# Attention and mixture of experts: key columns of z tile by tile, moving side in blocks of 32, stored squares read back in two transfers, other lags in the planner

## The chip, the cores and the metric

One core of one Trainium2 chip runs the kernel. The metric is the device time of one execution in microseconds (us). Before the change it is 2173.44 us, the median of three runs (2169.32 to 2173.81).

## The reference

Eight batches of 2496 tokens pass an attention without softmax and then a mixture of eight experts:

```python
scores = scale * np.matmul(z, z.transpose(0, 2, 1))      # scale = 1 / S, z is S x 64
attn = np.maximum(scores, 0.0) ** 2
out = np.matmul(attn, v)                                 # v is S x 256
x = (u * out).reshape(B * S, D)

logits = x @ w_gate + modality_bias[modality_id]
e_idx = np.argmax(logits, axis=1)                        # one expert a token
out[mask] = gate_w[mask, None] * (np.maximum(x[mask] @ w1[e], 0.0) @ w2[e])
```

Everything is single precision. The scores are symmetric, because both sides of the product are z.

## The kernel before

The kernel has two parts. The first does the attention of all batches and sends each token's row to a list of its expert in DRAM (`xs`). The second takes tiles of 512 rows from these lists and runs them through the expert's two matrices. The change touches only the first part, which ends about 1279 us into the span. Where single precision is wanted, a tile is split into a high and a low part (`ah` and `al`, `vh` and `vl`, the two halves of `zm`), and three matmuls are made of one.

**Tiles and steps.** A batch has 20 tiles of 128 keys and five chunks of queries, four of 512 and one of 448. A step (b, c, i) weighs the pair i of key tiles for query chunk c of batch b, so a chunk has ten steps and a batch fifty. Keys are grouped in chunks of four tiles as well. In a full step these instructions run:

- `scores` (L318): six matmuls on TensorE of 64 rows each, for two key tiles with three products of high and low parts. They are issued in pairs: the two of a pair use the two halves of the array's rows and run at the same time. The stationary side is 128 key columns of `zm`, given by `key_columns`; the moving side is the 512 query columns.
- `root` (L326) and `square` (L372) on ScalarE: the scores leave PSUM through a Relu and are squared, giving the tile `r`.
- `high` (L396) makes `ah` on ScalarE or VectorE, `low` (L405) makes `al` on VectorE.
- `weigh` (L429): 24 matmuls on TensorE, which add the squares times v to the chunk's four PSUM banks `acc` (two halves of the rows by two halves dh of the 256 columns). The first eight need `ah` and `vh`, the next `ah` and `vl`, the last `al` and `vh`.

**Squares used twice.** By symmetry, the squares of query chunk c and key chunk q with q > c are those of query chunk q and key chunk c, turned. So in a step whose keys lie in a later chunk, `turn_squares` (L343, VectorE) turns the 1024 elements in blocks of 32 x 32, and `store_squares` (L355, L359) sends them to DRAM in four transfers (six in the last pair). Later `load_turned` (L335) brings them back as the tile `r` of 158 steps, which then have no scores, root or square. A step of 242 in all has scores of its own.

**Key columns.** The host writes z with its tokens reordered. In the kernel before, two key tiles share 256 columns and alternate: tile j takes every second column. Only the last key chunk's third and fourth tile (pair i = 9) lie as 128 adjacent columns. The queries are read as 512 adjacent columns.

**The end of a chunk.** `evacuate_low` (L485, ScalarE) and `evacuate_high` (L489, VectorE) take the four `acc` banks into the rows tile `x`, multiplication by u follows (L496), then the rows are split in three bf16 parts `rb` (L508, L514, L510), turned on TensorE by `make_rows` (L525, two groups of 24 row-tiled pairs of short matmuls, in PSUM tiles `po`) and copied back (L535, L536). PSUM has two banks for one score tile and six others; four of the six hold `acc`, and the next chunk's first `weigh` needs four that the evacuation gives free. It is therefore made in two halves: first dh = 0, then dh = 1.

**What sets the order.** The whole first part is laid out by a planner in the kernel's Python code. Each piece of work has an engine, an assumed duration, a due time counted in steps (`need`), the pieces it comes after with a lag each (`after`), and the buffers that it takes and gives free. The planner walks the engines' assumed clocks and gives each engine the piece that is due first among those that are ready. The result is a fixed order on every engine. On the chip each engine then runs its list in order, and waits where an operand isn't there yet. All loads and stores of the first part go through one queue, issued by SyncE (SP), and each transfer waits for the one issued eight places earlier to have landed.

Of the kernel before, what the change touches and what calls it, by code (L numbers as in the profile page):

```python
# [11 lines left out]
I32 = mybir.dt.int32  # L12
# [15 lines left out]
def tile_attention_moe(ctx: ExitStack, tc: tile.TileContext, ut, v, zt, mid, wg, mb, w1, w2, out):  # L28
# [99 lines left out]
    n = NCOL - J  # L128
    nc.gpsimd.iota(toki[:, 0:n], pattern=[[T, NCH - 1], [1, J]], base=0, channel_multiplier=J)
    nc.gpsimd.iota(toki[:, n:NCOL - 1], pattern=[[1, J - 1]], base=n * P, channel_multiplier=J - 1)  # L130
# [64 lines left out]
    def load_modality():  # L195
        nc.sync.dma_start(out=brow, in_=mb.rearrange("(o m) e -> o m e", o=1).broadcast_to([P, 2, E]))
        mi = raw.tile([P, B, NCOL, 2], I32, tag="mi", name="mi")
        nc.gpsimd.memset(mi, 0)
        small_raw["mi"] = mi
        mid32 = mid.bitcast(I32).rearrange("(b s w) -> b s w", b=B, w=2)  # L200
        for c in range(NCH - 1):
            nc.sync.dma_start(
                out=mi[:, :, c * J:(c + 1) * J, :].rearrange("p b j w -> p b (j w)"),
                in_=mid32[:, c * T:(c + 1) * T, :].rearrange("b (p j) w -> p b (j w)", j=J),
            )
        c0, c1 = (NCH - 1) * J, NCOL - 1
        nc.sync.dma_start(
            out=mi[:, :, c0:c1, :].rearrange("p b j w -> p b (j w)"),
            in_=mid32[:, c0 * P:S - 64, :].rearrange("b (p j) w -> p b (j w)", j=J - 1),
        )  # L210
        nc.sync.dma_start(out=mi[0:64, :, c1, :], in_=mid32[:, S - 64:S, :].rearrange("b p w -> p b w"))

# [75 lines left out]
    steps = [(b, c, i) for b in range(B) for c in range(NCH) for i in order_of(b, c)]  # L288
    first_step = {(b, c): order_of(b, c)[0] for b in range(B) for c in range(NCH)}
    st_s, st_a, st_h, st_t = {}, {}, {}, {}  # L290
    acc = {}

    def key_columns(x, k):

        c, j = k // J, k % J
        if c == NCH - 1 and j >= J // 2:
            return x[:, j * P:(j + 1) * P]
        return x[:, j // 2 * H:(j // 2 + 1) * H].rearrange("p (k n) -> p n k", n=2)[:, j % 2]

# [4 lines left out]
    def scores(g, more=False):  # L304

        b, c, i = steps[g]
        w = width[c]
        if more:
            s = [bank_tile([P, T], "s") for _ in halves]
        else:  # L310
            both = ps_s.tile([P, 2, T], F32, tag="s", name="s")
            s = [both[:, t, :] for t in range(2)]
        mv = Z[b, c]
        for n, (kl, ql) in enumerate(((0, 1), (1, 0), (0, 0)) if g else ((0, 0), (0, 1), (1, 0))):
            for t in range(2):
                k = 2 * i + t
                lhs = key_columns(Z[b, k // J][halves[t], kl], k)
                nc.tensor.matmul(out=s[t][:, :w], lhsT=lhs, rhs=mv[halves[t], ql, :w], start=n == 0, stop=n == 2)  # L318
        st_s[g] = s if more or not g else both
# [9 lines left out]
    def load_turned(g):  # L329

        b, c, i = steps[g]
        w = width[c]
        a = bulk.tile([P, 2, T], F32, tag="a", bufs=NA, name="r")
        src = squares[i // 2, c, b % 2].rearrange("(s p k) q -> s p k q", s=2, k=2)
        nc.sync.dma_start(out=a[:, :, :w], in_=src[i % 2, :, :, :w])  # L335
        st_a[g] = a

    def turn_squares(g):

        b, c, i = steps[g]  # L340
        y = raw.tile([P, T // BLK, 2 * BLK], F32, tag="turn", bufs=2, name="turn")
        order = "p t (i n) -> p n t i" if i < NI - 1 else "p t (n i) -> p n t i"
        nc.vector.transpose(out=y.rearrange(order, n=2), in_=st_a[g].rearrange("p n (t i) -> p n t i", i=BLK))  # L343
        st_t[g] = y
# [173 lines left out]
    def make_rows(b, c, n):  # L518

        parts = turned_rows[b, c] = [bank_tile([P, J // 2, KD, DK + GW], "po") for _ in halves]  # L520
        for j in range(J // 2):
            for dh in range(KD):
                for m, x in enumerate(parted[b, c]):
                    for y, h in zip(parts, halves):
                        nc.tensor.matmul(  # L525
                            out=y[:, j, dh, :], lhsT=x[h, n * J // 2 + j, dh * P:(dh + 1) * P], rhs=mover[h, dh, :],
                            start=m == 0, stop=m == NP - 1,
                        )

    def take_rows(b, c, n, r):  # L530

        y = turned_rows[b, c][r]
# [368 lines left out]
    def piece(on, us, need, f, *args, after=(), take=(), drop=(), gate=-1):  # L901
        p = Piece(on, us, need, f, args, [d if isinstance(d, tuple) else (d, 0.1) for d in after if d], list(take), drop, gate)
        pieces.append(p)
        return p
# [26 lines left out]
    def z_pieces(b, c):  # L931
        need = uses_z[b, c][0] - LEAD
        read = None
        if b:
            hold_zr[b, c] = Hold("zr")
            read = transfer(0.7, need - 4, load_z, b, c, take=[hold_zr[b, c]], gate=need - 25)
        high = piece("A", 0.55, need - 1, prep_z_high, b, c, after=[read], take=[hold_z[b, c]], gate=int(need - 4))
        done_z[b, c] = piece("D", 0.65, need - 0.6, prep_z_low, b, c, after=[high], drop=[hold_zr[b, c]])
        begun.append(done_z[b, c])

    def v_pieces(b, c):
        need = uses_v[b, c][0]
        read = high = None
        if b or c == NCH - 1:
            if b:
                hold_vr[b, c] = Hold("vr")
            read = transfer(1.4, need - 5, load_v, b, c, issues=3 if c == NCH - 1 else 1, take=[hold_vr[b, c]], gate=need - 25)
        if (b, c) != (0, 1):
            high = piece("A", 0.95, need - 1.5, prep_v_high, b, c, after=[read], take=hold_v[b, c][:1])
        done_v[b, c] = piece("D", 1.15, need - 1.2, prep_v_low, b, c, after=[high], take=hold_v[b, c][1:], drop=[hold_vr[b, c]])  # L950
# [9 lines left out]
    def step_pieces(n):  # L960
# [4 lines left out]
        if is_turned(n):  # L965
            src = [stored[b, i // 2, 2 * c + k] for k in range(2)]
            p = transfer(1.4, n - LEAD - 2.5, load_turned, n, after=src, take=[hold_a], gate=n - LEAD - 4)
            high_after = (p, 0.2)
# [38 lines left out]
        if first and n:  # L1007
            p = piece("P", us / 2, n, weigh, n, 0, after=ready, take=own[0])
            p = piece("P", us / 2, n, weigh, n, 1, after=[(p, 0.0)], take=own[1], drop=hold_h + v_of)
        else:  # L1010
# [3 lines left out]

    acc_hold, later = {}, []

    def chunk_pieces(b, c):
# [7 lines left out]
        for h in range(KD):  # L1025
            lows.append(piece(
                "A", 0.5 * f + 0.06, end - 0.6, evacuate_low, b, c, h, after=[(w, 0.25)] + lows[:1], drop=[own[h][1]],
                take=[] if h else [hold_x[b, c]],
            ))
# [3 lines left out]
        for h in reversed(range(KD)):  # L1033
            highs.append(piece("D", 0.6 * f + 0.06, end - 0.4, evacuate_high, b, c, h, after=[lows[1]] + highs[:1], drop=[own[h][0]]))
        x = piece("D", 1.18, end + 1.5, weigh_u, b, c, after=[highs[1], read], drop=[hold_u[b, c]])
# [7 lines left out]
        for k in range(2):  # L1043
            own = [Hold("bank"), Hold("bank")]
            p = piece("P", 0.62, end + 3.4 + 0.3 * k, make_rows, b, c, k, after=[(p, 0.15), done_once["gate"]], take=own, drop=parts_of[:1] if k else [])
            took += [piece("A", 0.42, end + 3.6 + 0.3 * k, take_rows, b, c, k, r, after=[(p, 0.25)] + took[-1:], drop=own[r:r + 1]) for r in range(2)]
# [28 lines left out]
    done_once["gate"] = piece("D", 0.9, 7, prep_gate, after=[p])  # L1075
    p = transfer(2.0, 8, load_modality, issues=7, gate=6)
    done_once["modality"] = piece("D", 1.5, 20, prep_modality, after=[(p, 2.0)], gate=12)
# [416 lines left out]
```

## Time and profile before

| | |
|---|---|
| median of three runs | 2173.44 us (2169.32 to 2173.81) |
| profiled execution | 2171.07 us, span 2169.1 us |
| TensorE matmul busy | 2144.8 us (99%) |
| VectorE busy | 1653.8 us (76%) |
| ScalarE busy | 1456.9 us (67%) |
| granted TensorE clock | 0.998 |
| moved by DMA | 373.70 MB |

All views are of one execution. "Busy" for TensorE is the union of its matmuls, which overlap, so a busy engine can still be slower than it might be. A row of waits has the waiting engine, tile and line, what it waited for, and then the total in us, how often, and the longest. A row of the timeline has the start and the length in us, the engine (PE is TensorE's matmuls, PEld its weight loads, DVE VectorE, ACT ScalarE, POOL GpSimd, SPq the transfers issued by SP), the line, and how many instructions were merged. A row of the windows gives, for a stretch of the span, the busy time of PE, PEld, DVE, ACT and POOL with instruction counts, the granted clock, the busy share of the DMA engines, and GB/s. A row of grouped instructions ends with the count, the busy time in us and the mean of one in ns, and then the engine's idle time before them.

### The profile page before, as it was taken

The numbers are of one execution on the slowest core, as the hardware profiler recorded it, in microseconds if no ns is written. First come the engines' busy times: TensorE is split into PE (matmuls) and PEld (weight loads), VectorE is DVE, ScalarE is ACT, GpSimd is POOL, SyncE is SP. The second block draws the span as 40 slices with busy tenths as digits, with TensorE's granted clock in tenths as the row PEclk, the third lists the DMA queues.
The fourth block names the chain that finished last, engine by engine and source line by source line (L and its number), as shares of the span: only waits on it lengthen the run. The fifth ranks groups of instructions, "written<-read, shape, count | busy, mean of one in ns | idle before, by whom it ended". The sixth has DMA issues, their size and how long they took to land.

```text
span 2169.1 us, 44305 instructions
## 1 busy us (share of the span) xinstructions
PE 2144.8 (99%) x17190; PEld 1835.2 (85%) x17190; DVE 1653.8 (76%) x2260; ACT 1456.9 (67%) x2032; POOL 363.3 (17%) x342
## 2 busy tenths in 40 slices
PE   9999999999999999999999999999999999999997
PEld 7888888898889888888888988888888888888886
DVE  8888889789889788888788866666666666666664
ACT  8779779779778778778788653555455545555553
POOL 0000300300300301301302404121111212111121
PEclk9999999999999999999999999999999999999999
DMA  8976976967957957957957834554454535455450
GB/s 179 257 210 125 247 222 138 254 207 156 277 171 170 291 152 177 300 146 159 284 124 161 215 101 128 153 147 145 129 164 124 168 117 157 135 140 152 127 158 24
DMA packets 587878, 373.70 MB, mean 172 GB/s; under 512 B 488426, under 2 KB 543210, under 8 KB 581898
## 3 DMA queue, kind: packets, MB, share of 16 engines
q1 hardware_dynamic: 572570, 329.58, 59.3%
q0 software_dynamic: 15088, 41.21, 5.1%
q8 instruction: 136, 2.23, 0.4%
q14 instruction: 84, 0.69, 0.1%
HBM read 246.49 MB, written 140.96 MB: 179 GB/s over the span
## 4 chain that ended last, share of the span: by engine, by line
PE 48%; issue 26%; DMA 13%; DVE 4%; POOL 3%; SPq 3%; ACT 3%; POOLq 0%; DVEq 0%; ACTq 0%
PE acc L429 38%; DMA out_dram<-y,ids 10%; PE s L318 6%; POOL out_dram L1261 3%; PE po L525 2%; SPq L355 2%; DMA r<-squares 2%; PE ph L1238 1%; DVE al L405 1%; ACT r L326 1%; PE po L1251 1%; ACT r L372 1%; DMA squares<-turn 1%; DVE turn L343 1%; ACT ah L396 0%
## 5 line engine op out<-in xcount | busy, mean ns | idle before, releaser
L429 PE MATMUL acc<-ah,vh 64*128 64x512 f32 (+1 forms) x3120 | 455.3, 385 | 4.0 <-ACT x L485 3.1
L405 DVE TENSOR_TENSOR al<-r,ah 128x1024 fp32r<-128x1024 f32 (+1 forms) x359 | 422.2, 1187 | 36.0 <-ACT ah L396 30.3
L1251 PE MATMUL po<-w,hh 128*128 128x512 f32 x1248 | 445.8, 393 | 0.0
L429 PE MATMUL acc<-al,vh 64*128 64x512 f32 (+1 forms) x3120 | 443.9, 382 | 0.0
L429 PE MATMUL acc<-ah,vl 64*128 64x512 f32 (+1 forms) x3120 | 442.2, 382 | 0.0
L1242 ACT ACTIVATE hh<-ph 128x512 fp32r<-128x512 f32 x312 | 186.4, 597 | 376.8 <-PE ph L1238 337.0
L1238 PE MATMUL ph<-xh,w 128*128 128x512 f32 x1248 | 427.5, 393 | 0.0
L1243 DVE SCALAR_TENSOR_TENSOR hl<-ph,hh 128x512 fp32r<-128x512 f32 x312 | 215.7, 691 | 225.9 <-ACT hh L1242 192.7
L649 POOL DMA_INDIRECT xs<-x,sloti x160 | 205.6, 1285 | 1055.0 <-issue 501.7
L429 PEld LDWEIGHTS acc<-ah,vh 64*128 64x128 f32 x3120 | 319.8, 184 | 51.8 <-ACT x L485 5.4
L429 PEld LDWEIGHTS acc<-al,vh 64*128 64x128 f32 x3120 | 322.5, 184 | 41.9 <-DVE al L405 0.3
L429 PEld LDWEIGHTS acc<-ah,vl 64*128 64x128 f32 x3120 | 316.0, 184 | 42.8
L1252 PE MATMUL po<-w,hl 128*128 128x256 f32 x1248 | 348.6, 279 | 0.0
L396 ACT CAST ah<-r 128x1024 fp32r<-128x1024 f32 (+1 forms) x282 | 287.8, 1034 | 52.9 <-DMA r<-squares 28.5
L326 ACT ACTIVATE r<-s 128x1024 f32<-128x1024 f32 (+2 forms) x244 | 248.9, 1021 | 68.7 <-PE s L318 60.9
L1238 PEld LDWEIGHTS ph<-xh,w 128*128 128x128 f32 x1248 | 234.7, 188 | 54.0 <-PE acc L429 0.3
L1251 PEld LDWEIGHTS po<-w,hh 128*128 128x128 f32 x1248 | 234.3, 188 | 54.2
L1261 POOL DMA_INDIRECT out_dram<-y,ids x157 | 153.1, 975 | 741.0 <-DVE y L1289 702.6
L343 DVE STREAM_TRANSPOSE turn<-r 128x1024 f32<-128x1024 f32 x158 | 196.2, 1242 | 83.1 <-DMA squares<-turn 38.9
L372 ACT ACTIVATE r<-r 128x1024 f32<-128x1024 f32 (+2 forms) x243 | 255.7, 1053 | 5.4
L1238 PE MATMUL ph<-xl,w 128*128 128x512 f32 x624 | 245.6, 394 | 0.3 <-DVE xl L875 0.3
L1252 PEld LDWEIGHTS po<-w,hl 128*128 128x128 f32 x1248 | 234.2, 188 | 10.2 <-DVE hl L1243 0.3
(158 smaller groups left out, 2092.7 us busy)
## 6 DMA issues: line engine op xcount, KB each, us to landing
squares<-turn SPq DMA_DIRECT2D x508, 128.0 KB
r<-squares SPq DMA_DIRECT2D x96, 512.0 KB
w<-w1s SPq DMA_DIRECT2D x37, 1024.0 KB
w<-w2s SPq DMA_DIRECT2D x37, 1024.0 KB
r<-squares SPq DMA_DIRECT2D x62, 448.0 KB
ut<-in_ut_dram SPq DMA_DIRECT2D x40, 512.0 KB
xg<-xs SPq DMA_DIRECT2D x156, 128.0 KB
vr<-in_v_dram SPq DMA_DIRECT2D x32, 512.0 KB
```

The costliest lines, as they stand in the source:

```text
L326: nc.scalar.activation(out=r[:, t, :w], in_=s[t][:, :w] if g < 2 else s[:, :, :w], func=AF.Relu, scale=INV)
L343: nc.vector.transpose(out=y.rearrange(order, n=2), in_=st_a[g].rearrange("p n (t i) -> p n t i", i=BLK))
L372: nc.scalar.square(out=a[:, t, :w], in_=r[:, t, :w])
L396: copy(out=ah[:, :, :w], in_=st_a[g][:, :, :w])
L405: nc.vector.tensor_tensor(out=al[:, :, :w], in0=a[:, :, :w], in1=ah[:, :, :w].bitcast(F32), op=ALU.subtract)
L429: nc.tensor.matmul(out=acc[b, c][r][dh][:, :w], lhsT=V[b, k // J][y][halves[r], k % J, dh * P:(dh + 1) * P], rhs=x[halves[r], k % 2, :w], ...
L649: nc.gpsimd.indirect_dma_start(out=xs, out_offset=bass.IndirectOffsetOnAxis(ap=RT[b]["sloti"][:n, k:k + 1], axis=0), in_=x[:n, j, :], in_o ...
L1238: nc.tensor.matmul(out=ph, lhsT=lhs, rhs=rhs[:, k, :], start=n == 0, stop=n == 3 * KD - 1)
L1243: nc.vector.scalar_tensor_tensor(out=hl, in0=ph, scalar=0.0, in1=hh.bitcast(F32), op0=ALU.max, op1=ALU.subtract)
L1251: nc.tensor.matmul(out=po[j], lhsT=hh[:, s], rhs=both, start=f == 0, stop=False, skip_group_check=True)
L1252: nc.tensor.matmul(out=po[j][:, 0:D], lhsT=hl[:, s], rhs=w[:, 0, :], start=False, stop=f == KF - 1, skip_group_check=True)
L1261: nc.gpsimd.indirect_dma_start(out=out, out_offset=bass.IndirectOffsetOnAxis(ap=ids[:, j:j + 1], axis=0), in_=y, in_offset=None, bounds_ch ...
```

## The change

The host's order of z's columns within a chunk of 512 is new: the four key tiles lie one behind the other, 128 adjacent columns each. `key_columns` then reads adjacent columns for the key chunks 0 to 3; the first two tiles of the last key chunk stay interleaved. The queries of a chunk must come out in the order in which the keys are turned, so the moving side of the scores is now read in 16 blocks of 32 adjacent columns (`by_place`). With the queries' order, the order of u, of the modality ids (one prepared transfer instead of six) and of the token numbers changes, and `by_tile` reads the `acc` banks without a stride.

`turn_squares` writes each turned block as 32 adjacent columns except in pair 8; `store_squares` is unchanged. `load_turned` issues two transfers, one a key tile, where there was one.

In the planner, loads of z and v are due two steps earlier and the work on them is put 2.0 us after their landing rather than 0.1; the first group of `make_rows` is put 1.5 us after `rb` rather than 0.15, the second 0.1; the evacuations follow each other without a lag; and the second step of each chunk is weighed in two halves as the first is, its half dh = 0 due ahead of the first step's half dh = 1.

```diff
-        return x[:, j // 2 * H:(j // 2 + 1) * H].rearrange("p (k n) -> p n k", n=2)[:, j % 2]
+        if c < NCH - 1:
+            j = j % 2 * 2 + j // 2
+        elif j < J // 2:
+            return x[:, 0:H].rearrange("p (k n) -> p n k", n=2)[:, j]
+        return x[:, j * P:(j + 1) * P]
+
+    def by_place(c, x):
+        if c == NCH - 1:
+            return x[:, :LAST]
+        return x.rearrange("p (n a i) -> p a n i", n=2, i=BLK)
...
-                nc.tensor.matmul(out=s[t][:, :w], lhsT=lhs, rhs=mv[halves[t], ql, :w], start=n == 0, stop=n == 2)
+                rhs = by_place(c, mv[halves[t], ql])
+                nc.tensor.matmul(out=s[t][:, :w], lhsT=lhs, rhs=rhs, start=n == 0, stop=n == 2)
...
-        src = squares[i // 2, c, b % 2].rearrange("(s p k) q -> s p k q", s=2, k=2)
-        nc.sync.dma_start(out=a[:, :, :w], in_=src[i % 2, :, :, :w])
+        src = squares[i // 2, c, b % 2].rearrange("(s a k i) q -> s k a i q", s=2, k=2, i=BLK)
+        for k in range(2):
+            nc.sync.dma_start(out=a[:, k, :w], in_=src[i % 2, k, :, :, :w])
...
-        order = "p t (i n) -> p n t i" if i < NI - 1 else "p t (n i) -> p n t i"
+        order = "p t (i n) -> p n t i" if i == NI - 2 else "p t (n i) -> p n t i"
...
-            return [(y.rearrange("q (s p n) -> q s n p", s=2, n=2), x.rearrange("q (s n) p -> q s n p", s=2))]
+            return [(y.rearrange("q (j p) -> q j p", p=P), x)]
...
-            read = transfer(0.7, need - 4, load_z, b, c, take=[hold_zr[b, c]], gate=need - 25)
+            read = transfer(0.7, need - 6, load_z, b, c, take=[hold_zr[b, c]], gate=need - 25)
-        high = piece("A", 0.55, need - 1, prep_z_high, b, c, after=[read], ...
+        high = piece("A", 0.55, need - 1, prep_z_high, b, c, after=[(read, 2.0)], ...
...
-            p = transfer(1.4, n - LEAD - 2.5, load_turned, n, after=src, ...
+            p = transfer(1.4, n - LEAD - 2.5, load_turned, n, issues=2, after=src, ...
...
+        elif n > 1 and i == second_step[b, c] and i < NI - 1:
+            ready[-1] = (begun_chunk["half"], 0.0)
+            h = piece("P", us / 2, n - 0.95, weigh, n, 0, after=ready)
+            p = piece("P", us / 2, n, weigh, n, 1, after=[(h, 0.0), weighed["last"]], drop=hold_h + v_of)
...
-            p = piece("P", 0.62, ..., make_rows, b, c, k, after=[(p, 0.15), done_once["gate"]], ...
+            p = piece("P", 0.62, ..., make_rows, b, c, k, after=[(p, 0.1 if k else 1.5), done_once["gate"]], ...
```

The matmuls are the same in number; the planner's new lags and pieces move them. Three places show it. In the rows, L318 (before and after) is `scores`, L429 or L430 is `weigh`, L525 or L526 is `make_rows`; x4 three times is a half of a step, x8 three times a whole one.

The first place is TensorE at the start of the second query chunk of batch 0. Before:

```order
L318 MATMUL s<-zm 128x512 x6
L429 MATMUL acc<-ah,vh 128x512 x4
L429 MATMUL acc<-ah,vl 128x512 x4
L429 MATMUL acc<-al,vh 128x512 x4
L429 MATMUL acc<-ah,vh 128x512 x4
L429 MATMUL acc<-ah,vl 128x512 x4
L429 MATMUL acc<-al,vh 128x512 x4
L318 MATMUL s<-zm 128x512 x6
L429 MATMUL acc<-ah,vh 128x512 x8
```

And now:

```order
L318 MATMUL s<-zm 128x512 x6
L430 MATMUL acc<-ah,vh 128x512 x4
L430 MATMUL acc<-ah,vl 128x512 x4
L430 MATMUL acc<-al,vh 128x512 x4
L430 MATMUL acc<-ah,vh 128x512 x4
L430 MATMUL acc<-ah,vl 128x512 x4
L430 MATMUL acc<-al,vh 128x512 x4
L430 MATMUL acc<-ah,vh 128x512 x4
L430 MATMUL acc<-ah,vl 128x512 x4
L430 MATMUL acc<-al,vh 128x512 x4
L318 MATMUL s<-zm 128x512 x6
```

The middle half is the second step's dh = 0, which now stands between the two halves of the first step; the same holds at the start of every chunk but the first. The next score group, which came after two halves, comes after three.

The second place is TensorE in batch 3, from the end of the fourth query chunk's first halves to the `make_rows` of the chunk before it. Before:

```order
L429 MATMUL acc<-al,vh 128x512 x4
L429 MATMUL acc<-ah,vh 128x512 x8
L429 MATMUL acc<-ah,vl 128x512 x8
L429 MATMUL acc<-al,vh 128x512 x8
L429 MATMUL acc<-ah,vh 128x512 x8
L429 MATMUL acc<-ah,vl 128x512 x8
L429 MATMUL acc<-al,vh 128x512 x8
L429 MATMUL acc<-ah,vh 128x512 x8
L429 MATMUL acc<-ah,vl 128x512 x8
L429 MATMUL acc<-al,vh 128x512 x8
L525 LDWEIGHTS rb
L525 MATMUL po<-mover,rb 128x88
```

And now:

```order
L430 MATMUL acc<-al,vh 128x512 x4
L430 MATMUL acc<-ah,vh 128x512 x8
L430 MATMUL acc<-ah,vl 128x512 x8
L430 MATMUL acc<-al,vh 128x512 x8
L430 MATMUL acc<-ah,vh 128x512 x8
L430 MATMUL acc<-ah,vl 128x512 x8
L430 MATMUL acc<-al,vh 128x512 x8
L318 MATMUL s<-zm 128x512 x6
L430 MATMUL acc<-ah,vh 128x512 x8
L430 MATMUL acc<-ah,vl 128x512 x8
L430 MATMUL acc<-al,vh 128x512 x8
L526 LDWEIGHTS rb
```

Counted from the chunk's first matmul, 96 matmuls of `weigh` stood ahead of `make_rows`, and now 120 do, one whole step more (its second step is now in two halves ahead of these rows). For the rows of the third chunk this is so in batches 0 to 5, while batches 6 and 7 keep their place; for those of the first chunk the count goes from 120 to 144 in batches 0 to 3 and 7.

The third place is SP's queue in the first batch, around the first load of stored squares (in `squares_1_0` the 1 is the later of the two chunks and the 0 the batch's parity). Before:

```order
L355 DMA squares_2_0_80<-turn 32x16x64 x8
L335 DMA r<-squares_1_0_64 128x1024
L196 DMA brow<-in_moe_modality_bias_dram 128x16
L202 DMA mi<-in_moe_modality_id_dram 128x8x8 x4
L207 DMA mi<-in_moe_modality_id_dram 128x8x6
L211 DMA mi<-in_moe_modality_id_dram 64x8x2
L355 DMA squares_3_0_74<-turn 32x16x64 x8
```

And now:

```order
L356 DMA squares_2_0_80<-turn 32x16x64 x8
L336 DMA r<-squares_1_0_64 128x1x512 x2
L199 DMA brow<-in_moe_modality_bias_dram 128x16
L201 DMA mi<-in_moe_modality_id_dram 128x320
L356 DMA squares_3_0_74<-turn 32x16x64 x8
```

Every load of stored squares takes two places of the queue, and the modality ids one instead of six.

More of the change, by code (lines that the diff above doesn't have):

```diff
@@ L128, in tile_attention_moe @@
     n = NCOL - J
-    nc.gpsimd.iota(toki[:, 0:n], pattern=[[T, NCH - 1], [1, J]], base=0, channel_multiplier=J)
+    for k in range(P // BLK):
+        mine = slice(k * BLK, (k + 1) * BLK)
+        at = lambda m: m * BLK * (k // 2) + k % 2
+        nc.gpsimd.iota(toki[mine, 0:n], pattern=[[T, NCH - 1], [2, 2], [J * DK, 2]], base=at(J), channel_multiplier=J)
     nc.gpsimd.iota(toki[:, n:NCOL - 1], pattern=[[1, J - 1]], base=n * P, channel_multiplier=J - 1)
@@ L197, in load_modality @@
         mi = raw.tile([P, B, NCOL, 2], I32, tag="mi", name="mi")
-        nc.gpsimd.memset(mi, 0)
+        nc.sync.dma_start(out=mi, in_=mid.bitcast(I32).rearrange("p (b j w) -> p b j w", b=B, w=2))
         small_raw["mi"] = mi
[L200 to L211, printed above, removed]
     def prep_modality():
@@ L518, in make_rows @@
     def make_rows(b, c, n):
-        parts = turned_rows[b, c] = [bank_tile([P, J // 2, KD, DK + GW], "po") for _ in halves]
+        parts = turned_rows[b, c, n] = [bank_tile([P, J // 2, KD, DK + GW], "po") for _ in halves]
         for j in range(J // 2):
@@ L901, in piece @@
     def piece(on, us, need, f, *args, after=(), take=(), drop=(), gate=-1):
-        p = Piece(on, us, need, f, args, [d if isinstance(d, tuple) else (d, 0.1) for d in after if d], list(take), drop, gate)
+        p = Piece(on, us, need, f, args, [d for d in (d if isinstance(d, tuple) else (d, 0.1) for d in after) if d[0]], list(take), drop, gate)
         pieces.append(p)
@@ L935, in z_pieces @@
             hold_zr[b, c] = Hold("zr")
-            read = transfer(0.7, need - 4, load_z, b, c, take=[hold_zr[b, c]], gate=need - 25)
-        high = piece("A", 0.55, need - 1, prep_z_high, b, c, after=[read], take=[hold_z[b, c]], gate=int(need - 4))
+            read = transfer(0.7, need - 6, load_z, b, c, take=[hold_zr[b, c]], gate=need - 25)
+        high = piece("A", 0.55, need - 1, prep_z_high, b, c, after=[(read, 2.0)], take=[hold_z[b, c]], gate=int(need - 4))
         done_z[b, c] = piece("D", 0.65, need - 0.6, prep_z_low, b, c, after=[high], drop=[hold_zr[b, c]])
@@ L946, in v_pieces @@
                 hold_vr[b, c] = Hold("vr")
-            read = transfer(1.4, need - 5, load_v, b, c, issues=3 if c == NCH - 1 else 1, take=[hold_vr[b, c]], gate=need - 25)
+            read = transfer(1.4, need - 7, load_v, b, c, issues=3 if c == NCH - 1 else 1, take=[hold_vr[b, c]], gate=need - 25)
         if (b, c) != (0, 1):
-            high = piece("A", 0.95, need - 1.5, prep_v_high, b, c, after=[read], take=hold_v[b, c][:1])
+            high = piece("A", 0.95, need - 1.5, prep_v_high, b, c, after=[(read, 2.0)], take=hold_v[b, c][:1])
         done_v[b, c] = piece("D", 1.15, need - 1.2, prep_v_low, b, c, after=[high], take=hold_v[b, c][1:], drop=[hold_vr[b, c]])
@@ L966, in step_pieces @@
             src = [stored[b, i // 2, 2 * c + k] for k in range(2)]
-            p = transfer(1.4, n - LEAD - 2.5, load_turned, n, after=src, take=[hold_a], gate=n - LEAD - 4)
+            p = transfer(1.4, n - LEAD - 2.5, load_turned, n, issues=2, after=src, take=[hold_a], gate=n - LEAD - 4)
             high_after = (p, 0.2)
@@ L1007, in step_pieces @@
         if first and n:
-            p = piece("P", us / 2, n, weigh, n, 0, after=ready, take=own[0])
-            p = piece("P", us / 2, n, weigh, n, 1, after=[(p, 0.0)], take=own[1], drop=hold_h + v_of)
+            p = begun_chunk["half"] = piece("P", us / 2, n, weigh, n, 0, after=ready, take=own[0])
+            p = piece("P", us / 2, n + 0.1, weigh, n, 1, after=[(p, 0.0)], take=own[1], drop=hold_h + v_of)
+        elif n > 1 and i == second_step[b, c] and i < NI - 1:
+            ready[-1] = (begun_chunk["half"], 0.0)
+            h = piece("P", us / 2, n - 0.95, weigh, n, 0, after=ready)
+            p = piece("P", us / 2, n, weigh, n, 1, after=[(h, 0.0), weighed["last"]], drop=hold_h + v_of)
         else:
@@ L1013, in step_pieces @@
         p.step = n
-    acc_hold, later = {}, []
+    acc_hold, later, begun_chunk = {}, [], {}
     def chunk_pieces(b, c):
@@ L1026, in chunk_pieces @@
             lows.append(piece(
-                "A", 0.5 * f + 0.06, end - 0.6, evacuate_low, b, c, h, after=[(w, 0.25)] + lows[:1], drop=[own[h][1]],
+                "A", 0.5 * f + 0.06, end - 0.6, evacuate_low, b, c, h, after=[(w, 0.25)] + [(p, 0.0) for p in lows], drop=[own[h][1]],
                 take=[] if h else [hold_x[b, c]],
@@ L1033, in chunk_pieces @@
         for h in reversed(range(KD)):
-            highs.append(piece("D", 0.6 * f + 0.06, end - 0.4, evacuate_high, b, c, h, after=[lows[1]] + highs[:1], drop=[own[h][0]]))
+            highs.append(piece("D", 0.6 * f + 0.06, end - 0.4, evacuate_high, b, c, h, after=[lows[1]] + [(p, 0.0) for p in highs], drop=[own[h][0]]))
         x = piece("D", 1.18, end + 1.5, weigh_u, b, c, after=[highs[1], read], drop=[hold_u[b, c]])
@@ L1044, in chunk_pieces @@
             own = [Hold("bank"), Hold("bank")]
-            p = piece("P", 0.62, end + 3.4 + 0.3 * k, make_rows, b, c, k, after=[(p, 0.15), done_once["gate"]], take=own, drop=parts_of[:1] if k else [])
+            p = piece("P", 0.62, end + 3.4 + 0.3 * k, make_rows, b, c, k, after=[(p, 0.1 if k else 1.5), done_once["gate"]], take=own, drop=parts_of[:1] if k else [])
             took += [piece("A", 0.42, end + 3.6 + 0.3 * k, take_rows, b, c, k, r, after=[(p, 0.25)] + took[-1:], drop=own[r:r + 1]) for r in range(2)]
```

22 lines of the change are left out of this document (9 added, 13 removed).

## The prediction

> **What bounds the kernel now.** The page's first lines come first, then the windows of three stretches: the first part, the second part, and the tail after the last tile.
>
> ```profile
> span 2169.1 us, 44305 instructions
> PE 2144.8 (99%) x17190; PEld 1835.2 (85%) x17190; DVE 1653.8 (76%) x2260; ACT 1456.9 (67%) x2032; POOL 363.3 (17%) x342
> ...
> 0.00:1279.00 1279.00, 1267.98 (x12736) 1095.71 (x12736) 1074.09 (x1438) 1017.40 (x1360) 198.56 (x173) 1.00 0.78 199
> 1279.00:2150.00 871.00, 870.70 (x4423) 734.35 (x4420) 576.39 (x815) 436.19 (x667) 160.87 (x165) 1.00 0.47 135
> ```
>
> TensorE is the bound throughout, at a granted clock of 1.00. In the second part its matmuls cover 870.7 of 871 us and the change doesn't touch it. In the first part 11.0 of 1279 us are uncovered. So the change can gain in two ways only: part of those 11 us, or matmuls that follow one another faster. The waits of TensorE say what the uncovered time is:
>
> ```profile
> PE po L525 <- DVE rb L510: 3.7, 6, 1.0
> PE acc L429 <- ACT x L485: 3.1, 4, 1.1
> PE s L318 <- ACT r L326: 2.0, 2, 1.5
> PE warm L1115 <- POOL zeros L102: 1.0, 1, 1.0
> PE acc L429 <- DVE ah L379: 0.7, 1, 0.7
> ```
>
> Two rows carry 6.8 us: `make_rows` comes before its last bf16 part is there, and the second half of a chunk's first step comes before ScalarE has emptied the banks. The others belong mainly to the first microseconds. For the second way, TensorE's timeline in the first chunk of the first batch shows score groups between whole steps:
>
> ```profile
> 26.70 0.86 PE L318 MATMUL s<-zm 64*128 64x512 f32 x6
> 27.40 1.07 PE L429 MATMUL acc<-ah,vh 64*128 64x512 f32 x8
> 28.31 1.07 PE L429 MATMUL acc<-ah,vl 64*128 64x512 f32 x8
> 29.22 1.07 PE L429 MATMUL acc<-al,vh 64*128 64x512 f32 x8
> 30.13 0.86 PE L318 MATMUL s<-zm 64*128 64x512 f32 x6
> 30.83 1.07 PE L429 MATMUL acc<-ah,vh 64*128 64x512 f32 x8
> ...
> 33.55 0.84 PE L318 MATMUL s<-zm 64*128 64x512 f32 x6
> 34.23 1.07 PE L429 MATMUL acc<-ah,vh 64*128 64x512 f32 x8
> ```
>
> The groups that start at 26.70 and 30.13 read their keys in every second column and take 0.70 us until the next matmul starts. The group at 33.55 is pair 9, whose keys are adjacent already, and takes 0.68. A whole step of `weigh` takes 2.73 (27.40 to 30.13).
>
> **Keys tile by tile: -3.2 us.** The number of score groups comes from the rows of grouped instructions:
>
> ```profile
> L318 PE MATMUL s<-zm 64*128 64x512 f32 x1344 | 204.3, 399 | 2.1 <-ACT r L326 2.0
> L318 PE MATMUL s<-zm 64*128 64x448 f32 x108 | 14.9, 373 | 0.0
> ```
>
> These are 1452 matmuls, 242 groups of six. Each of the 40 chunks has one group of pair 8, which stays interleaved, and one of pair 9, which was adjacent before. 162 groups are left, and 162 x 0.02 = 3.2 us. The page Advanced Engine Details and Errata of the Trainium skill, section SBUF Cachelines, says that an access pattern loses nothing as long as it hits each 16-byte line at least twice. A column of every two in single precision does so, and by that rule the keys would give 0 and the whole sum 3.2 us less gain. The rows differ from the rule by a little, 0.70 against 0.68.
>
> **Moving side in blocks of 32: 0.** No row shows a moving side in blocks. A gain is excluded, since all moving sides of before are adjacent. Above, the nearest row is the loss of a strided stationary side, 0.02 us a group: over the 224 groups of 512 queries (1344 / 6) that is 4.5 us. I take 0, because a block is 32 adjacent columns and the strided row breaks at every column.
>
> **`make_rows` later: -3.1 us.** By the order, the rows that have waited in the third chunk's place come one whole step later in six of eight batches, those of the first chunk in five. A step is 2.73 us and the longest wait is 1.0, so a wait whose group moves is gone. I take five of the six as moved: 5/6 x 3.7 = 3.1. The step that goes ahead must have its `ah` and `al` ready that much earlier; it followed at once before, and no row shows TensorE waiting for `al`.
>
> **Second step in halves: -2.6 us.** The wait looks like this on TensorE, 1.12 us for ScalarE's copy out of the bank:
>
> ```profile
> 427.02 0.72 PE L429 MATMUL acc<-al,vh 64*128 64x512 f32 x4
> 427.48 0.96 PE L318 MATMUL s<-zm 64*128 64x512 f32 x6
> 428.18 0.39 PE L429 MATMUL acc<-ah,vh 64*128 64x512 f32 x1
> 429.69 0.73 PE L429 MATMUL acc<-ah,vh 64*128 64x512 f32 x3 [1.12 <-ACT x L485]
> ```
>
> A score group of 0.70 us stood between the halves; now a half step stands there, 2.73 / 2 = 1.36, and at some chunks the score group as well. So each of the four waits shrinks by at least 0.66: 4 x 0.66 = 2.6, at most all 3.1. What is late next is that half's own operands, needed 1.4 us earlier; that is in the last term.
>
> **Evacuation and turning without a stride: 0.** Two pairs of rows compare strided with adjacent work of the same size:
>
> ```profile
> L485 ACT COPY x<-acc 128x512 f32<-128x512 f32 x64 | 36.3, 586 | 26.4 <-PE acc L429 26.2
> L1242 ACT ACTIVATE hh<-ph 128x512 fp32r<-128x512 f32 x312 | 186.4, 597 | 376.8 <-PE ph L1238 337.0
> L343 DVE STREAM_TRANSPOSE turn<-r 128x1024 f32<-128x1024 f32 x158 | 196.2, 1242 | 83.1 <-DMA squares<-turn 38.9 <-ACT r L372 33.8 <-issue 5.1
> L863 DVE STREAM_TRANSPOSE xt<-xg 128x1024 f32<-128x1024 f32 x39 | 48.2, 1237 | 0.0
> ```
>
> ScalarE reads a bank with a stride in 586 ns and without in 597; VectorE turns with interleaved output in 1242 and with adjacent output in 1237. At most 158 x 5 ns = 0.8 us of VectorE are in it, off the path.
>
> **Two transfers for one load: 0.** The row of these issues and the waits behind them:
>
> ```profile
> L335 SPq DMA_DIRECT2D r<-squares x158: 319/542/2585, 32.8 to 1250.7; - x158
> ...
> ACT ah L396 <- DMA r<-squares: 28.5, 17, 3.6
> ```
>
> SP issues 158 more, 158 x 0.542 = 86 us over 1250, and each takes one of the eight places in flight, so stores and loads of z, v and u queued behind are issued about half a microsecond later. ScalarE already waits 28.5 us for these loads, and of that nothing stands as such in TensorE's rows; some of it stands in the 3.1 us above, because the copy out of the bank was queued behind a waiting `ah`. The cover is that a load is issued several steps before it is weighed. If it is gone, the price is the same row doubled once where it reaches TensorE, 3.1 us. For the other direction, two halves that land separately can't be used separately, since `ah` reads both; I take 0 and keep 0 to 3.1. The page DMA: Bandwidth & Descriptors of the Trainium skill, section Bandwidth, advises transfers of 1 MiB and more and fits about 2 us of fixed time to each. The 158 more would be 316 us by that, which the eight in flight spread; no run here separates it yet. The other loads' earlier due times and the single transfer of modality ids act on ScalarE's waits alone and count as 0.
>
> **New waits: +3.0 us.** The planner's order changed everywhere, and its clocks are assumptions, which is why the waits above exist. I charge as much as the rows of `make_rows` give back, 3.1 rounded, between 0 (every new place fits) and 8.9 (every gain comes back).
>
> **The sum.** -3.2 - 3.1 - 2.6 + 3.0 = -5.9. The profiled execution took 2171.07 us, 2.0 outside its span, which stays; it becomes 2165.2. It lies 2.4 below the median of the three runs, 2173.44, so I add half of that: 2166.4.
>
> **The rivals.** *The waits come back.* New waits of the planner's order eat 6 us or more of the 8.9, or blocks of 32 cost their 4.5. For it: 5 of the 11 us lie in a dozen places where the assumed clock missed the chip's. Against it: the moved groups have more than twice the margin of their longest wait. Time: 2172.3 (the midpoint of profiled run and median) less 0 to 3, so 2171.
>
> *Slower: the lead of the score chain runs out in the first chunk of each batch.* There the other engines are full too:
>
> ```profile
> 16.00:28.00 12.00, 12.00 (x108) 9.93 (x106) 12.00 (x13) 11.87 (x14) 0.00 (x0) 1.00 0.77 153
> ...
> DVE al L405 <- ACT ah L396: 30.3, 26, 3.5
> ```
>
> VectorE is busy 12.00 of 12 us and ScalarE 11.87. By the order a score group has slid behind a half step at a chunk's start, so fewer scores are ahead when the steps that need them come. VectorE waits for `ah` 26 times, 30.3 us, 1.17 each, and none of it reaches TensorE, because the scores run ahead. If half of it did, 15 us come on top: 2166.4 + 15 = 2181. It decides where the lead is shorter than score, root, square, `ah` and `al` together. Against it: a group that is one place later has lost about one step of several.
>
> *The page's rule holds.* If stride two is free as the cacheline rule has it, the 0.02 us a group come from elsewhere and stay, and the sum is -2.7: 2169.6. The rows speak against it: 0.70 and 0.68 lie in the same timeline, 7 us apart.
>
> **How the numbers follow.** The forecast gets 0.57, the waits that come back 0.22, the lost lead 0.15, the free stride 0.06. About 0.2%, 4.3 us, is what a measurement of this kernel can tell from no change. Faster by more, below 2169.1, is the forecast alone: 0.57. Within 0.2% are the second and the fourth: 0.28. Slower is the third: 0.15. The range goes down to all of 3.2 + 3.7 + 3.1 + 2.0 = 12.0 gained with no new wait, 2159, less a microsecond for the scatter of the runs: 2158. It goes up to the slow rival at three quarters of its price: 2178. The forecast's own range is 2160 to 2169.
>
> **What would show it.** Right: between whole steps a score group with 512 queries and keys 0 to 3 takes 0.68 us until the next matmul; the row of `po` waiting for `rb` falls to about 0.6 us and that of `acc` waiting for `x` to about 0.5; `r<-squares` has 316 issues; the second part still takes 871 us. Blocks of 32 at a price: 0.70 or more there, and pair 9, which was 0.68, gets slower. The slow rival: rows of TensorE waiting for `al` or `ah` in the first chunk of the batches, many and short. A step is wrong if the new waits on TensorE together exceed 6 us, or if `acc` waits for `ah` or `al` of the second step where it waited for `x`.

## The result, and the profile after

The changed kernel takes 2645.17 us, the median of five runs (2642.86 to 2648.57), against 2173.44 us before. The ratio is 1.2177, with a 95% interval of 1.2162 to 1.2191. The forecast of 2166.4 us is wrong by far, on the other side and outside its range.

The first lines of the page of the changed kernel, its slices, and the windows of the first and the second part (for each stretch, the busy time of PE, PEld, DVE, ACT and POOL, the granted clock, the DMA share and GB/s):

```profile
span 2644.4 us, 44515 instructions
...
PE 2291.9 (87%) x17190; PEld 1937.1 (73%) x17190; DVE 1663.9 (63%) x2263; ACT 1447.1 (55%) x2029; POOL 361.7 (14%) x344
...
PE   9778877976986886797698788789999999999998
...
PEclk9888988987998897898799889899999999999999
DMA  7655654764575565476456546535444454455541
...
0.00:1279.00 1279.00, 1024.24 (x9168) 863.27 (x9170) 787.97 (x1025) 732.36 (x983) 134.14 (x125) 0.89 0.60 149
1279.00:1760.00 481.00, 396.18 (x3595) 338.31 (x3592) 300.66 (x427) 278.15 (x383) 62.80 (x50) 0.90 0.55 135
1760.00:2620.00 860.00, 859.71 (x4371) 725.56 (x4370) 570.32 (x802) 430.99 (x654) 159.87 (x164) 1.00 0.48 136
```

The span is 475 us longer. The second part is as before, 859.7 of 860 us covered. All of the loss is in the first part, which now lasts until about 1755 us instead of 1279 (the last `weigh` ends there). TensorE's uncovered time went from 24.3 us to 352.5 (2644.4 - 2291.9), which is 328 us. The other 147 us are covered time: the same 17190 matmuls take longer, at a granted clock of 0.89 where it was 1.00. An estimate by the clock alone fits: the 1268 us of matmuls of the first part, divided by 0.89, are 1425, and 1420 were measured. VectorE and ScalarE work as long as before, so they have idle time. And the DMA engines, which had a busy share of 0.78 in the first part, have 0.60. Nothing looks overloaded, and everything waits.

What for is said by the waits. First those of all engines, then TensorE's own:

```profile
ACT ah L397 <- DMA r<-squares: 439.3, 82, 14.9
...
DVE al L406 <- ACT ah L397: 267.8, 100, 8.3
...
DVE ah L397 <- DMA r<-squares: 141.2, 34, 8.4
...
PE po L526 <- ACT rb L537: 137.5, 47, 12.7
DVE turn L344 <- DMA squares<-turn: 88.8, 46, 6.2
...
PE acc L430 <- DVE ah L397: 42.4, 10, 9.1
PE acc L430 <- DVE al L406: 41.9, 18, 5.9
PE acc L430 <- ACT ah L397: 40.0, 13, 6.8
PE po L526 <- DVE rb L511: 36.9, 11, 6.0
PE s L318 <- ACT r L326: 21.3, 13, 5.1
```

`ah` on ScalarE waited 28.5 us for the loads of stored squares before, and waits 439.3 now; VectorE's `ah` adds 141.2. TensorE's waits go along with these: of its 339 us of waits in the first part, ScalarE or VectorE stands in front of such a load at the same moment in 175. The rest is put down to work that queued up behind, which is argued and not counted. One place of ScalarE's timeline shows how:

```profile
293.89 0.26 ACT L537 COPY rb<-po 128x96 f32<-128x96 f32 x1
300.91 1.04 ACT L397 CAST ah<-r 128x1024 fp32r<-128x1024 f32 x1 [6.76 <-DMA r<-squares]
301.87 1.02 ACT L326 ACTIVATE r<-s 128x1024 f32<-128x1024 f32 x1
...
302.93 1.65 PE L318 MATMUL s<-zm 64*128 64x512 f32 x6 [4.02 <-ACT r L326]
```

ScalarE sits 6.76 us in front of `ah`. The root behind it in its queue gets its turn only then, and TensorE waits 4.02 us for that root to free the score banks. The last fence line is TensorE's.

The transfers themselves hold the clue. The trace has a record of each DMA packet, and for the packets of 1792, 2048 and 4096 bytes (those of the loads of squares, and of other transfers whose packets have these sizes) one can add up the time in which exactly so many were on their way:

```
packets in flight at once     2        4     15 to 17
before                     43 us    29 us     257 us
after                      77 us   611 us     114 us
```

Before, about 16 at once is the most common state of these packets. Now it is four, by far (633 us when the packets of 4096 bytes, which the loads no longer have, are left out). The packets' records don't name their engine, but the landings tell the same. A transfer's semaphore is a counter that is raised as its parts land; that of a load was raised 16 times before (119 of 158 loads) and five times now (281 of 316). From a load's issue to its last raise it took 5.3 us before and takes 8.7 now (medians).

### The profile page after: what moved, and what is told of

Read it like the earlier page. It is cut to its first block, busy times and chain, and to the rows that moved or that the text cites. A ratio compares the mean times of both kernels' runs of the same rounds, so it can differ in the third digit from the quotient of the medians.

```text
span 2644.4 us, 44515 instructions
## 1 busy us (share of the span) xinstructions
PE 2291.9 (87%) x17190; PEld 1937.1 (73%) x17190; DVE 1663.9 (63%) x2263; ACT 1447.1 (55%) x2029; POOL 361.7 (14%) x344
## 5 line engine op out<-in xcount | busy, mean ns | idle before, releaser
L430 PE MATMUL acc<-ah,vh 64*128 64x512 f32 (+1 forms) x3120 | 512.0, 418 | 85.7 <-DVE ah L397 42.4
L397 ACT CAST ah<-r 128x1024 fp32r<-128x1024 f32 (+1 forms) x279 | 287.8, 1034 | 471.5 <-DMA r<-squares 439.3
L430 PE MATMUL acc<-al,vh 64*128 64x512 f32 (+1 forms) x3120 | 476.4, 398 | 45.0 <-DVE al L406 41.9
L430 PE MATMUL acc<-ah,vl 64*128 64x512 f32 (+1 forms) x3120 | 479.1, 403 | 0.0
L430 PEld LDWEIGHTS acc<-ah,vh 64*128 64x128 f32 x3120 | 350.7, 203 | 146.3 <-DVE ah L397 47.1
L430 PEld LDWEIGHTS acc<-al,vh 64*128 64x128 f32 x3120 | 338.4, 194 | 102.7 <-DVE al L406 52.8
L430 PEld LDWEIGHTS acc<-ah,vl 64*128 64x128 f32 x3120 | 345.6, 200 | 46.2
L318 PE MATMUL s<-zm 64*128 64x512 f32 (+1 forms) x1452 | 240.5, 427 | 21.4 <-ACT r L326 21.3
L344 DVE STREAM_TRANSPOSE turn<-r 128x1024 f32<-128x1024 f32 x158 | 195.7, 1240 | 100.5 <-DMA squares<-turn 88.8
```

What stands on the lines that cost most here:

```text
L318: nc.tensor.matmul(out=s[t][:, :w], lhsT=lhs, rhs=rhs, start=n == 0, stop=n == 2)
L397: copy(out=ah[:, :, :w], in_=st_a[g][:, :, :w])
L430: nc.tensor.matmul(out=acc[b, c][r][dh][:, :w], lhsT=V[b, k // J][y][halves[r], k % J, dh * P:(dh + 1) * P], rhs=x[halves[r], k % 2, :w], ...
```

## Experiments

**Theory A:** a load runs on as many of the 16 DMA engines as the slowest dimension of its source allows. `"(s a k i) q -> s k a i q"` gives a source of 4 groups by 32 rows, so it is four engines, always the same four, and they are the bound of the first part. **Theory B:** twice as many transfers fill the queue and its eight places. **Theory C:** the planner's new order lost the lead of the score chain (the slow rival of the prediction). Two pairs of kernels separate them, and more runs then take the rest of the change apart.

**Four transfers by partitions.** Twice as many transfers again, but with 32 rows as the slowest dimension of the source.

```diff
-        src = squares[i // 2, c, b % 2].rearrange("(s a k i) q -> s k a i q", s=2, k=2, i=BLK)
-        for k in range(2):
-            nc.sync.dma_start(out=a[:, k, :w], in_=src[i % 2, k, :, :, :w])
+        src = squares[i // 2, c, b % 2].rearrange("(s a k i) q -> s a i k q", s=2, k=2, i=BLK)
+        for n in range(P // BLK):
+            nc.sync.dma_start(out=a[n * BLK:(n + 1) * BLK, :, :w], in_=src[i % 2, n, :, :, :w])
```

The planner is told of four issues, here and in the next run.

> The changed kernel, but each load of stored squares is four transfers, one for 32 partitions and both key tiles, so that the slowest dimension of its source is 32 rows and not the 4 groups of rows. Theory A (the load runs on as many of the 16 DMA engines as divide its slowest dimension, 4 in the changed kernel; in its trace these packets are 633 us long exactly four at a time): 16 engines carry it again and the time falls to 2165 to 2190 us. Theory B (twice as many transfers fill the queue and its eight places): there are twice as many again, so it is slower than 2645, some 2800. Theory C (the planner's new order lost the lead of the scores): 2645 within 20, since the order is nearly the same. The Trainium skill's page DMA: Bandwidth & Descriptors, section Why a DMA increments its semaphore by 16 and not by 1, has the rule of theory A.

Measured: 2217.79 us, ratio 1.0201 to before (1.0180 to 1.0222). More transfers and 427 us less. The waits for the loads are down to a seventh on ScalarE:

```profile
ACT ah L397 <- DMA r<-squares: 63.9, 35, 5.9
...
DVE ah L397 <- DMA r<-squares: 20.3, 12, 4.9
```

Theory B and C fall as causes of the 22%. But 2217.79 is also above the 2165 to 2190 that A expected, so a smaller part, of the number of transfers or of something that goes with it, is left.

**Four transfers on two engines.** The same number and size of transfers as the last, but the slowest dimension of the source is 2.

```diff
+        for n in range(4):
+            k, h = n // 2, n % 2
+            nc.sync.dma_start(out=a[halves[h], k, :w], in_=src[i % 2, k, 2 * h:2 * h + 2, :, :w])
```

> The same count and size of transfers as the four by partitions, and the changed kernel otherwise, but each has a source whose slowest dimension is 2. Theory A: two engines carry all loads. 45568 packets of about 94 ns are 2140 us on each of two, and the stores add some 400, so the first part takes about 2500 instead of 1770 and the whole 3200 to 3500 us. Theory B: the same as the four by partitions, within 1%. Theory C: 2645 within 20.

Measured: 3390.45 us, ratio 1.5598 (1.5569 to 1.5626). The table's row for it: exactly two packets in flight for 1420 us, four for 25, 15 to 17 for 109; with four transfers by partitions it was 38, 32 and 204. The page and waits of this kernel:

```profile
span 3387.8 us, 45091 instructions
...
PE 2404.6 (71%) x17190; PEld 2004.6 (59%) x17190; DVE 1673.1 (49%) x2278; ACT 1438.9 (42%) x2014; POOL 354.9 (10%) x344
...
ACT ah L398 <- DMA r<-squares: 994.6, 92, 29.0
```

The two kernels issue equally many transfers of the same size and differ in the shape of each: 32 rows by both key tiles into 32 partitions, or 2 groups of 32 rows of one tile into 64 partitions. They take 2218 and 3390 us. The partitions don't explain it, since 128 of them went with 16 packets at a time before and with four in the changed kernel, and 32 with about 16 again. The landings agree: the semaphore of a load is raised 16 times by partitions (486 of 632 loads) and three times here (611 of 632), once more than the engines of theory A both here and in the changed kernel. Theory A is shown.

Its size fits too. In the changed kernel's first part the packets of the loads (15872 of 1792 bytes, and 24576 of the 29696 of 2048; the other 5120 are there before as well and belong to other loads) take about 3760 us together, 940 on each of four engines. All other packets take 12640, or 790 on each of 16 if they spread evenly, an estimate. That is 1730 of 1755 us. For two engines the same sum gives 1770 + 790 = 2560, and the first part took 2498. (The expectation above counted the 5120 among the loads.) That they are always the same four is seen from the pairs. In the changed kernel SP issues the two loads of a step one right after the other:

```profile
291.68 1.22 SPq L336 DMA_DIRECT2D r<-squares  x2
```

Each needs 32 packets of about 0.1 us on each of its four engines, some 3 us, so on different engines eight packets would often be in flight.

**Two loads in the kernel before.** One part of the change alone, in the layout of before, where the slowest dimension stays 128.

```diff
+        for k in range(2):
+            nc.sync.dma_start(out=a[:, k, :w], in_=src[i % 2, :, k, :w])
...
-            p = transfer(1.4, n - LEAD - 2.5, load_turned, n, after=src, ...
+            p = transfer(1.4, n - LEAD - 2.5, load_turned, n, issues=2, after=src, ...
```

> The kernel before with its loads of stored squares split into two transfers, one a key tile, of 128 rows each, so that the slowest dimension stays 128. Nothing else differs but the planner's count of issues. Theory A: all 16 engines, 2165 to 2185 us, within 0.5% of before. Theory B: the larger part of the loss is here, 2400 or more. Theory C: within 0.5% of before.

Measured: 2190.43 us, ratio 1.0070 (1.0050 to 1.0091), above the 2185 that A expected at most. Two transfers are not free, 0.7%, and not the loss of 22% either.

**The same with the order of before.** The planner isn't told of the second issue.

> The kernel before with two loads of 128 rows for one, and the planner still told of one issue, so that the order on every engine is that of before. If the second transfer itself made the 0.7% of the two loads with the planner told, it is 2185 to 2195 us again. If it was the order that the planner made for two issues, it is 2170 to 2178, that of before.

Measured: 2185.22 us, ratio 1.0051 (1.0032 to 1.0070). So the second transfer itself costs most of it, together with its shorter packets: with 512 queries they have 2048 bytes where those of the one load have 4096. TensorE's waits:

```profile
PE acc L430 <- ACT x L486: 6.6, 7, 2.1
PE po L526 <- DVE rb L511: 4.2, 6, 1.2
PE acc L430 <- ACT ah L397: 2.4, 1, 2.4
PE s L318 <- ACT r L326: 1.5, 1, 1.5
```

The wait for the copy out of the bank doubles, 3.1 to 6.6. That fits the chain that the prediction named (a load that lands late, `ah` behind it, the copy behind that), and ScalarE's wait for the loads grows from 28.5 to 35.6 us. But TensorE's uncovered time in the first part grows by only 6.4 of the 13.9 us that this part gets longer; the rest is matmuls that take longer. In all it is 158 transfers for 12.3 us (2185.22 - 2172.88), 0.08 us each; the four by partitions have 474 more than one load has and take 49 us more than the kernel with one load below (2217.79 - 2168.70), 0.10 each. What of it is SP's time to issue, what the eight places and what the shorter packets wasn't separated.

**The planner's part alone**, in the kernel before.

> The kernel before with the planner's part of the change alone: lags, due times, the second step in halves. Layouts, loads and modality ids as before. Theory A: no loss; by the terms of the forecast the waits for rb and for the banks lose 5.7 us and new ones cost up to 3, so 2163 to 2175. Theory B: the same. Theory C: the loss is here, 2400 or more.

Measured: 2165.57 us, ratio 0.9967 (0.9951 to 0.9983), faster than before and than the changed kernel, and the fastest of those that do the whole computation. TensorE's waits in it, all of them:

```profile
PE s L318 <- ACT r L326: 2.2, 2, 1.5
PE po L525 <- ACT rb L536: 1.1, 5, 0.3
PE warm L1119 <- POOL zeros L102: 1.0, 1, 1.0
PE acc L429 <- DVE al L405: 0.8, 3, 0.4
PE acc L429 <- DVE ah L396: 0.7, 2, 0.5
PE ph L1242 <- DVE xl L875: 0.3, 1, 0.3
```

The two rows of 3.7 and 3.1 us are gone, and waits of 0.8 (`acc` for `al`) and 1.1 (`po` for the copy of `rb`) have come. Theory C falls.

**One load again.** The whole change, but the stored squares' rows lie in an order that one load reads with 128 rows as slowest dimension, and the planner is told of one issue.

```diff
-        src = squares[i // 2, c, b % 2].rearrange("(s a k i) q -> s k a i q", s=2, k=2, i=BLK)
-        for k in range(2):
-            nc.sync.dma_start(out=a[:, k, :w], in_=src[i % 2, k, :, :, :w])
+        src = squares[i // 2, c, b % 2].rearrange("(s k p) q -> s p k q", s=2, k=2)
+        nc.sync.dma_start(out=a[:, :, :w], in_=src[i % 2, :, :, :w])
...
-        order = "p t (i n) -> p n t i" if i == NI - 2 else "p t (n i) -> p n t i"
-        nc.vector.transpose(out=y.rearrange(order, n=2), in_=st_a[g].rearrange("p n (t i) -> p n t i", i=BLK))
+        halves_of = "p (s m a) (i n) -> p s n a m i" if i == NI - 2 else "p (s m a) (n i) -> p s n a m i"
+        to = y.rearrange(halves_of, s=2, m=2, n=2)
+        of = st_a[g].rearrange("p n (s a m i) -> p s n a m i", s=2, m=2, i=BLK)
+        for s in range(2):
+            nc.vector.transpose(out=to[:, s], in_=of[:, s])
```

> The changed kernel with all its layouts and lags, except that the turned blocks go to DRAM in an order of rows that one load can read with 128 rows as slowest dimension; the turning takes two instructions for it, some 0.2 us more of VectorE in 158 steps. Theory A (the engines that carry the load are the whole loss): within 0.5% of the kernel before with the new lags alone, 2160 to 2180 us, and score groups of 0.70 us. Rival (something else in the layouts, reading in blocks or the turned order, costs too): above 2190.

Measured: 2168.70 us, ratio 0.9986 (0.9975 to 0.9997). With the load on all engines the other parts of the change together are 0.14% faster than before. They are 3.1 us slower than the planner's part alone, but the two intervals overlap, so that the layouts lose a little is likely and not shown by the time.

**Keys and moving side, each alone**, on top of the planner's part. The columns belong to other tokens than the rest of the kernel takes them for, as the expectations say, so the results are other numbers. The work is the same: 17190 matmuls, and a second part of 890.0 us in both kernels, as against 889.8 before.

```diff
+        if c < NCH - 1 or j >= J // 2:
+            return x[:, j * P:(j + 1) * P]
```

> The kernel before with the new lags, and the key columns of key chunks 0 to 3 read as 128 adjacent columns without the host's order changed, so that other tokens' scores are computed; the moving side stays adjacent. If adjacent keys are worth 0.02 us a group as the forecast took it, the score groups between whole steps take 0.68 us and the time is about 3 us below that of the new lags alone, 2160 to 2166. If stride two is free as the Trainium skill's cacheline rule has it, 0.70 us stay.

```diff
+                if c < NCH - 1:
+                    rhs = rhs.rearrange("p (n a i) -> p a n i", n=2, i=BLK)
```

> The kernel before with the new lags and strided keys, and the moving side read in 16 blocks of 32 columns without the host's order changed, so that the columns of the scores are in another order than the rest takes them for. If blocks cost 0.02 us a group beside what strided keys cost, groups take 0.72 us and the time is 4.5 us above that of the new lags alone. If the slower of the two sides sets the pace, they stay at 0.70 us and the time is the same. If blocks are free, also 0.70, and then the changed kernel's groups should have been 0.68, which they weren't.

Measured: 2164.38 us with adjacent keys (ratio 0.9954, 0.9937 to 0.9970) and 2170.36 with blocks (0.9986, 0.9975 to 0.9996), beside 2165.57 with neither. TensorE's timeline, first adjacent keys with an adjacent moving side:

```profile
26.59 0.84 PE L318 MATMUL s<-zm 64*128 64x512 f32 x6
27.27 1.07 PE L429 MATMUL acc<-ah,vh 64*128 64x512 f32 x8
28.18 1.07 PE L429 MATMUL acc<-ah,vl 64*128 64x512 f32 x8
```

then strided keys with blocks, and last adjacent keys with blocks (the kernel with one load again):

```profile
30.03 0.87 PE L321 MATMUL s<-zm 64*128 64x512 f32 x6
30.73 1.09 PE L432 MATMUL acc<-ah,vh 64*128 64x512 f32 x8
31.66 1.08 PE L432 MATMUL acc<-ah,vl 64*128 64x512 f32 x8
```

```profile
26.25 0.87 PE L318 MATMUL s<-zm 64*128 64x512 f32 x6
26.96 1.09 PE L432 MATMUL acc<-ah,vh 64*128 64x512 f32 x8
27.89 1.07 PE L432 MATMUL acc<-ah,vl 64*128 64x512 f32 x8
```

A group takes 0.68 us with both sides adjacent, 0.70 with strided keys (the prediction's rows), and 0.70 to 0.71 with blocks, whichever way the keys lie. The eight matmuls behind it take 0.91 us after an adjacent moving side and 0.93 after blocks. So blocks undo what adjacent keys gain, and cost 0.02 more in the next eight: 224 x 0.02 = 4.5 us, measured 4.8 (2170.36 - 2165.57), though the two intervals overlap a little. No case of the expectation for blocks came whole: the groups stay at 0.70, as for the slower side setting the pace, and the time rises by what the first case gave, in matmuls that it didn't name. The gain of the keys is seen in the rows; in the time its 1.2 us are within the intervals.

## Why the prediction was wrong, point by point

**Two transfers for one load: 0, "keep 0 to 3.1".** This step failed, and it is the whole of the wrong answer. It counted issues, bytes and places in the queue, and put the number of engines that carry a load at what it was without a word on it. It didn't look at the order of the new source's dimensions, though the changed line spells it out: `s k a i q` with a = 4. The price is not 0 to 3.1 us but 476.5, the difference between the changed kernel and its copy with one load (2645.17 - 2168.70). The kernel lost 471.7 against before, so this is all of it, and the other parts together gain the small rest. None of the rivals had it. The Trainium skill's page DMA: Bandwidth & Descriptors, section Why a DMA increments its semaphore by 16 and not by 1, gives the rule: the number of engines is the largest up to 16 that divides the slowest dimension of both sides. The traces agree, with four packets in flight where it is 4, two where it is 2, and about 16 where it is 32 or 128; no run here has a size that would tell "divides" from "is not above". The prediction cited the same page of the Trainium skill for the size of transfers, and missed this section. The 2 us of fixed time that it took from there stand in another section, Anatomy of one DMA, fitted for transfers issued from GpSimd, while these are issued by SP; here the second transfer on all engines cost 0.08 us. The trace of before doesn't show that such a load would use four engines, but it would have given the price once that was known: its loads take about 3900 us of packets, 970 on each of four engines, beside some 750 of other traffic on each (0.78 of 1279 us less the loads' sixteenth). That is over 1700 us where the first part had 1279.

**What bounds the kernel.** Right for before, wrong as a bound on the change. That only 11 us were uncovered limits a gain; it says nothing of a loss.

**`make_rows` later, second step in halves: -3.1 and -2.6, new waits +3.0.** The mechanism was right. Both rows vanished altogether in the kernel with the planner's part alone. The new waits were mis-sized: 0.8 and 1.1 us instead of 3.0. This part measured -7.2 us (2172.79 to 2165.57; by its interval -3.7 to -10.6) where the terms gave -2.7. (The "5 of the 11 us in a dozen places", with which the prediction weighs the waits coming back, are 6.8 us in ten by its own rows.) TensorE's uncovered time in the first part fell from 11.0 to 6.4 us, which is 4.6 of it; the rest is not in waits and lies within the interval. The slow rival of the lost lead didn't happen.

**Keys tile by tile: -3.2.** Right in the rows, 0.70 to 0.68, and not to be told from nothing in the time. But the term was added as if it were independent of the next.

**Moving side in blocks: 0, up to 4.5.** Wrong; the upper end was the value, 4.5 by rows and 4.8 by time, and on top the groups lose what adjacent keys would give. The reason given, that a block breaks only every 32 columns, doesn't hold. Why blocks cost as much as a stride in every column stays open. The rule that the prediction weighed, of the Trainium skill's page Advanced Engine Details and Errata, section SBUF Cachelines, would have both free, and neither row agrees.

**Evacuation and turning: 0.** Nothing measured contradicts it: the turning takes 1240 ns in the changed kernel, and 1242 before, and ScalarE's copy out of a bank 593 and 586.

**What would show it.** Several of the signs named there came up at once in the changed kernel: new waits far above 6 us, waits for `ah` and `al` (up to 9.1 us long, and not short as for the lost lead), groups at 0.70, and pair 9 slower. Pair 9 of the first chunk, which took 0.68 us before:

```profile
33.44 0.87 PE L318 MATMUL s<-zm 64*128 64x512 f32 x6
34.14 1.09 PE L430 MATMUL acc<-ah,vh 64*128 64x512 f32 x8
```

But the sign for this cause, time from issue to landing or packets in flight, wasn't among them.

## What to carry to other kernels

When a transfer's access pattern changes, write down the sizes of its dimensions from the slowest to the fastest, for both sides, before anything else is counted: a slowest dimension of 4 in place of 128 cost this kernel 22%. Waits for one kind of transfer that grow while the mean DMA share falls are the sign of it; a mean over 16 engines hides four full ones. And a change of several parts is worth taking apart even when it loses: here the lags alone are 0.33% faster than before.

## What the runs showed of the hardware that was not expected

- The granted clock was lower the more TensorE waited. With 11 us uncovered in the first part (before) it was 1.00 there, with 45 (four by partitions) 0.99, with 340 (the changed kernel) 0.89, and with 970 (four on two engines) 0.78. In the changed kernel 147 of the 475 us are matmuls that took longer: each matmul of `weigh`'s first eight took 418 ns in place of 385. That the waits cause it wasn't tried by itself; in the second part, almost without waits, the clock is 1.00 again in the same run.
- Loads on a few engines hold up other transfers too, though not all alike. VectorE's turning waited 38.9 us for its stores before, 88.8 in the changed kernel and 184.8 with two engines, though the stores themselves are unchanged. From issue to landing the loads of u took 4.8, 10.2 and 12.1 us (medians), those of v 5.3, 4.7 and 5.4, the stores 3.9, 4.1 and 3.9. SP's own time to issue the 694 stores grew from 495 to 762 us in the changed kernel. What of it is the full engines and what the eight places of the queue wasn't separated.
- An additional transfer costs this kernel 0.08 to 0.10 us even when it runs on all engines and carries no more bytes. Its packets are shorter for most loads, and that wasn't tried apart.
